# A third of the key sums moved from VectorE to accumulating DMAs of GpSimd's queue

## The chip, the cores and the metric

One core of a Trainium2 chip runs the kernel. Its engines work side by side and meet at semaphores: TensorE (PE; its weight loads are PEld), VectorE (DVE), ScalarE (ACT), GpSimd (POOL) and SyncE (SP), which here only issues DMAs. The metric is the device time of one execution in microseconds (us); smaller is better.

## The reference

Attention with a soft cap over 4 batches of 12 heads, 448 positions and 64 channels a head, and a mixer behind it. Cut to what matters:

```python
scores = scale * q @ k.T
scores = cap * tanh(scores / cap)
attn = exp(scores - max);  attn = attn / sum(attn)      # over keys
x = attn @ v                                            # heads side by side: 448 x 768
h = relu(x.T @ w_tok1) @ w_tok2;  u = x + h.T           # mixes positions
out = u + relu(u @ w_ch1) @ w_ch2                       # mixes channels
```

All is float32.

## The kernel before

Attention takes two heads (a pair `p`) at a time, with keys in the partitions. The 448 keys are cut into three full chunks of 128 (`c` = 0, 1, 2) and one of 64 (`c` = 3); the 64-key chunks of an even pair and of the odd pair after it are packed into one tile. So two pairs have seven units of work, and the 24 pairs have 84. A unit is: the score matmuls (`qk_unit`, L182 or L188), one tanh (L195) and one exponential (L200) of a 128 x 896 tile `e` on ACT, and the matmuls with v (`pv_full` L217, `pv_packed` L226).

The exponentials must also be summed over keys. `add_up` does it in two moves: DVE first adds the chunks of a pair elementwise into `acc` (128 x 2 x 448 for each of two pairs), and later `add_rows` lets PE add up the 128 partitions with a matmul by ones (L265). In `add_up`, chunk 0 + chunk 1 make `acc` (L239), chunk 2 is added in place (L245), and the packed chunk is added as two halves of 64 partitions (`add_packed`, L257). For an odd pair the packed chunk, which has been there since the even pair, is added right behind L239, before chunk 2.

The order is written out by hand. There are 42 steps with two units each. Step `t` issues the v matmuls of its own two units, then the scores, tanh and exponentials of the two units of step `t + 2`, then `add_up` for its own units, then some 1.8 us (as the program reckons) of background PE work, taken from a list: `add_rows` of two pairs, and the first half of the mixer for batches that are done (transposes L326, `tok1` L353, `tok2` L373). `at(d, f)` puts `f` off by `d` steps. Behind `add_rows` comes a chain with one step for each link: copy the sums out of PSUM (L270), gather them by DMA (L286), reciprocal (L290), store and spread them by DMA (L292, L299), and scale the pair's output (`scale_pair`, L303), which the transposes read. After attention, `while accs` makes steps without new units until the last sums are issued; then the second half of the mixer (`ch1` L552, `ch2` L569) fills the rest, with the last of the background work put between its matmuls.

Three pools of buffers tie this together. `e` has 8 buffers, so the tanh of unit `n` overwrites the tile of unit `n - 8`, and waits for all that read that tile. `acc` has 2 buffers of two pairs each. The score PSUM tile has 2 buffers. GpSimd's only steady work is a subtraction in the decoding of weights (L119), and no DMA is issued from its queue. DVE's other work in this stage is weight decoding (L99 to L116), copies out of PSUM (L270, L279) and the differences of the high and low parts (L339, L340, L362, L439).

Of the kernel before, what the change touches and what calls it, by code (L numbers as in the profile page):

```python
# [12 lines left out]
ALU = mybir.AluOpType  # L13
# [26 lines left out]
def tile_softcap_mixer(ctx, tc, qk, v, cap, w1, w2, wc1, wc2, out):  # L40
    nc = tc.nc
# [30 lines left out]
    def at(d, f, y=0):  # L72
        later.setdefault((now[0] + d, y), []).append(f)
# [80 lines left out]
    def half(i, j):  # L154
        return slice((i ^ j) * D, ((i ^ j) + 1) * D)
# [18 lines left out]
    es = {}  # L174
# [55 lines left out]
    accs = {}  # L230

    def add_up(b, p, c):
        q, i = divmod(p, 2)
        if c == 0:
            return
        if c == 1:
            if i == 0:
                accs[b, q] = pe.tile([P, 2, 2, S], F32, tag="acc", name="acc", bufs=2)
            nc.vector.tensor_tensor(accs[b, q][:, i], es.pop((b, p, 0)), es.pop((b, p, 1)), op=ALU.add)  # L239
            if i == 1:  # L240
                add_packed(b, p)
                es.pop((b, p - 1, NF))
        elif c == 2:
            t = accs[b, q][:, i]
            nc.vector.tensor_tensor(t, t, es.pop((b, p, 2)), op=ALU.add)  # L245
            if i == 1:
                left[b] += 1
                at(1, lambda: work.insert(0, (add_rows(b, q), lambda: True)))
        else:
            add_packed(b, p)  # L250

    def add_packed(b, p):
        q, i = divmod(p, 2)
        for j in range(2):
            r = half(i, j)
            t = accs[b, q][r, i, j]
            nc.vector.tensor_tensor(t, t, es[b, p - i, NF][r, i], op=ALU.add)  # L257

    def add_rows(b, q):
        ps = ps_c.tile([P, 512], F32, tag="c", name="ps_s")  # L260
        acc = accs.pop((b, q))
        for i in range(2):
            for j in range(2):
                r = (2 * i + j) * SP
                nc.tensor.matmul(ps[r:r + SP, :S], ones, acc[:, i, j], start=True, stop=True, tile_position=(0, r))  # L265
        yield 750, True

        def take():
            x = px.tile([P, S], F32, tag="xs", name="xs", bufs=1)
            nc.vector.tensor_copy(x, ps[:, :S])  # L270
            at(pace[0], lambda: gather(b, q, x))

        read_at(b, None, take)
# [8 lines left out]
    def gather(b, q, x):  # L282
        s = px.tile([P, S // SP], F32, tag="sums", name="sums", bufs=1)
        for i in range(4):
            r = slice(i * SP, (i + 1) * SP)
            nc.sync.dma_start(s[r], x[i * SP:i * SP + 1, :].rearrange("p (a c) -> p a c", a=SP))  # L286
        at(pace[0], lambda: norm(b, q, s), 1)
# [112 lines left out]
    work = []  # L400
# [3 lines left out]
    def read_at(b, f, g):  # L404
        def free():
            unread[0] -= 1
            left[b] -= 1

        if f is not None:
            at(1, f)  # L410
        at(1, g, 1)
        at(slack[0], free, 0 if slack[0] > 1 else 1)
# [80 lines left out]
    for t in range(steps_in):  # L493
# [11 lines left out]
        for b, p, c in two:  # L505
            add_up(b, p, c)
            n = pairs.index((b, p))
            if c == (2 if p % 2 else NF) and n + 3 < len(pairs):
                at(1, lambda n=n: load_v(*pairs[n + 3]))
            if b == 0 and c == 1 and tokw_steps:  # L510
                tokw_steps.pop(0)()
            if b >= 1 and p % 2 and c == 2 and w0_steps:
                w0_steps.pop(0)()
# [238 lines left out]
```

## Time and profile before

| | |
|---|---|
| Device time, 3 runs | median 607.08 us (605.6 to 607.22) |
| The profiled execution | 605.01 us, of which the span of the profile is 603.0 us |
| Granted TensorE clock | 1.00 over the whole span |
| PE, DVE, ACT, POOL busy | 592.0, 384.9, 254.5, 54.5 us |

The span runs from the first to the last instruction; 2.0 us of the profiled execution lie outside it. A "<-" behind a row's idle time names what the engine was waiting for. A busy share says how much of a stretch an engine had work in it, not whether that work was waited for.

### The profile page before, as it was taken

How to read it: one execution, taken by the hardware profiler on the slowest of the kernel's cores; microseconds unless marked ns; L12 is line 12 of the kernel's file. 1: busy time of each engine (PE TensorE's matmuls, PEld its weight loads, DVE VectorE, ACT ScalarE, POOL GpSimd, SP SyncE). 2: the span in 40 equal slices, each digit the busy share in tenths (PEclk: the TensorE clock that was granted, in tenths of full speed). 3: DMA queues.
4: the chain of work that ended last, by engine and by line, in shares of the span. 5: the costliest groups of instructions: out<-in, count | busy, mean ns of one | idle time of the engine just before them, and what ended most of it. 6: DMA issues, size and time to landing. Idle time of an engine off the chain costs nothing.

```text
span 603.0 us, 7760 instructions
## 1 busy us (share of the span) xinstructions
PE 592.0 (98%) x3012; PEld 438.2 (73%) x3012; DVE 384.9 (64%) x626; ACT 254.5 (42%) x330; POOL 54.5 (9%) x48
## 2 busy tenths in 40 slices
PE   8998999999999999999999999999999999999997
PEld 2232444444444589997999999999989999999986
DVE  2899879696996996547788386438643853333324
ACT  7998987888878733114332122012211220000000
POOL 0021000000010000002331022001200120000000
PEclk9999999999999999999999999999999999999999
DMA  6545434244442201001343121202120200000224
GB/s 202 170 127 160 148 123 152 78 158 144 135 156 81 68 31 32 0 1 36 104 124 123 34 70 59 83 0 76 66 70 1 70 1 1 1 1 0 93 100 180
DMA packets 24620, 49.12 MB, mean 81 GB/s; under 512 B 6784, under 2 KB 16512, under 8 KB 24576
## 3 DMA queue, kind: packets, MB, share of 16 engines
q1 hardware_dynamic: 24288, 48.37, 24.9%
q8 instruction: 25, 0.41, 0.3%
q14 instruction: 19, 0.16, 0.1%
q10 hardware_dynamic: 288, 0.18, 0.1%
HBM read 42.86 MB, written 5.59 MB: 80 GB/s over the span
## 4 chain that ended last, share of the span: by engine, by line
PE 89%; DVE 5%; ACT 3%; issue 1%; DMA 1%; POOL 0%; SPq 0%; DVEq 0%
PE ps_g L552 29%; PE ps_o L569 29%; PE ps_pv L217 8%; PE ps_qk L182 8%; PE ps_h L353 5%; PE ps_u L373 5%; PE ps_s L265 2%; PE ps_pv L226 2%; PE ps_qk L188 1%; PE ps_t L326 1%; ACT e L195 1%; DVE acc L257 1%; ACT e L200 1%; DVE acc L239 1%; DMA qkraw<-in_qk 1%
## 5 line engine op out<-in xcount | busy, mean ns | idle before, releaser
L569 PE MATMUL ps_o<-g,wc 128*128 128x448 f32 x864 | 182.7, 367 | 0.0
L569 PEld LDWEIGHTS ps_o<-g,wc 128*128 128x128 f32 x864 | 161.6, 188 | 15.2 <-DVE u L574 0.9
L552 PE MATMUL ps_g<-uhl,wc 128*128 128x448 f32 x648 | 138.4, 367 | 0.0
L552 PEld LDWEIGHTS ps_g<-uhl,wc 128*128 128x128 f32 x648 | 120.9, 188 | 10.3
L574 DVE TENSOR_TENSOR u<-u,ps_o 128x448 f32<-128x448 f32 (+1 forms) x145 | 86.7, 612 | 46.8 <-PE ps_o L569 46.6
L195 ACT ACTIVATE e<-ps_qk,tsc 128x896 f32<-128x896 f32 x84 | 81.1, 1022 | 27.9 <-PE ps_qk L182 25.5
L200 ACT ACTIVATE e<-e,near 128x896 f32<-128x896 f32 x84 | 83.5, 1057 | 0.0
L119 POOL TENSOR_TENSOR wc<-wz,wc 128x512 fp32r<-128x512 f32 x36 | 48.2, 1341 | 385.4 <-ACT wc L118 361.9
L557 ACT ACTIVATE g<-ps_g 128x896 fp32r<-128x896 f32 x24 | 22.0, 916 | 142.5 <-PE ps_g L552 142.5
L558 DVE SCALAR_TENSOR_TENSOR g<-ps_g,g 128x896 fp32r<-128x896 f32 x24 | 26.1, 1088 | 75.1 <-ACT g L557 75.1
L182 PE MATMUL ps_qk<-qkraw 64*128 64x448 f32 x288 | 66.1, 570 | 1.0 <-DMA qkraw<-in_qk 0.9
L217 PE MATMUL ps_pv<-e,vn 128*64 128x448 f32 x288 | 64.2, 556 | 0.5 <-ACT e L195 0.5
L182 PEld LDWEIGHTS ps_qk<-qkraw 64*128 64x128 f32 x288 | 24.0, 186 | 42.9 <-issue 12.1
L118 ACT ACTIVATE wc<-wz 128x512 fp32r<-128x512 f32 x36 | 22.7, 629 | 74.6 <-PE ps_g L552 33.9
L552 PE MATMUL ps_g<-last_u,wc 128*128 128x448 f32 x216 | 45.6, 367 | 0.4 <-PE ps_o L569 0.3
L552 PEld LDWEIGHTS ps_g<-last_u,wc 128*128 128x128 f32 x216 | 40.4, 188 | 4.7 <-issue 0.7
L104 ACT ACTIVATE wz<-wraw 128x512 f32<-128x512 f32 x36 | 24.2, 673 | 46.1 <-DMA wraw<-in_wc 27.9
L217 PEld LDWEIGHTS ps_pv<-e,vn 128*64 128x64 f32 x288 | 16.5, 135 | 33.4 <-issue 15.9
L107 DVE TENSOR_SCALAR wz<-wz 128x512 f32<-128x512 f32 (+1 forms) x40 | 17.4, 435 | 34.8 <-ACT wz L104 34.7
L353 PEld LDWEIGHTS ps_h<-wc,last_u 128*128 128x128 f32 x176 | 30.4, 188 | 8.0 <-issue 6.0
L353 PE MATMUL ps_h<-wc,last_u 128*128 128x384 f32 x176 | 36.0, 343 | 0.0
L373 PE MATMUL ps_u<-last_u,wc 128*128 128x448 f32 x144 | 34.1, 375 | 1.5 <-DVE wc L362 0.8
(50 smaller groups left out, 414.3 us busy)
## 6 DMA issues: line engine op xcount, KB each, us to landing
wraw<-in_wc SPq DMA_DIRECT2D x36, 512.0 KB, 3.6
qkraw<-in_qk SPq DMA_DIRECT2D x23, 448.0 KB, 3.3
vn<-in_v SPq DMA_DIRECT2D x24, 224.0 KB, 3.4
rb<-rs SPq DMA_DIRECT2D x48, 112.0 KB, 2.8
out_t<-u SPq DMA_DIRECT2D x23, 224.0 KB, 1.9
wraw<-in_w SPq DMA_DIRECT2D x2, 512.0 KB, 4.7
wraw<-in_w SPq DMA_DIRECT2D x2, 448.0 KB, 3.7
sums<-xs SPq DMA_DIRECT2D x48, 1.8 KB, 2.3
```

What stands on the lines that cost most here:

```text
L104: nc.scalar.activation(zf, bits(r[:, :, 1]), AF.Abs, scale=2.0 ** -16)
L119: nc.gpsimd.tensor_tensor(lo, zf, hi, op=ALU.subtract)
L182: nc.tensor.matmul(ps[:, j, :S], raw[r, 1, c * P:(c + 1) * P], raw[r, 0], start=True, stop=True)
L195: nc.scalar.activation(e, scores.pop((b, p, c))[:, :, :S], AF.Tanh, scale=tsc)
L200: nc.scalar.activation(e, e, AF.Exp, scale=near)
L217: nc.tensor.matmul(ps[j * D:(j + 1) * D, :S], vn[p % 3][:, j * NF + c], es[b, p, c][:, j], start=first, stop=last)
L353: nc.tensor.matmul(ps[:, :HALF], w, x, start=(n == 0), stop=(n == len(mm) - 1))
L373: nc.tensor.matmul(ps[:, :S], h1[:, hi, t, cs], w2s[:, wi, t, :], start=(n == 0), stop=(n == 3 * NT - 1))
L552: nc.tensor.matmul(ps[:, i, :S], w[:, wi, cc, fs], uhl[b][:, ui, cc, :], start=(n == 0), stop=(n == 3 * NC - 1))
L558: nc.vector.scalar_tensor_tensor(g[:, 1], ps[:, :, :S], 0.0, g[:, 0], op0=ALU.max, op1=ALU.subtract)
L569: nc.tensor.matmul(ps[:, :S], w[:, wi, i, cs], g[:, gi, i, :], start=(n == 0), stop=(n == 3 * GF - 1))
L574: nc.vector.tensor_tensor(u[b][:, cc, r], u[b][:, cc, r], ps[:, r], op=ALU.add)
```

## The change

The third key chunk of each pair is no longer added by DVE (L245). A DMA issued from GpSimd's queue reads the 128 x 896 tile `e`, adds it to `acc` and writes `acc` (`accum_op=ALU.add`). For an odd pair it is issued where L245 stood; for an even pair it is issued one unit later, behind the packed chunk's two additions. `add_rows` is put into the list two steps after the odd pair's third chunk, where it was one step.

```diff
         elif c == 2:
-            t = accs[b, q][:, i]
-            nc.vector.tensor_tensor(t, t, es.pop((b, p, 2)), op=ALU.add)
             if i == 1:
+                add_third(b, p)
                 left[b] += 1
-                at(1, lambda: work.insert(0, (add_rows(b, q), lambda: True)))
+                at(2, lambda: work.insert(0, (add_rows(b, q), lambda: True)))
         else:
             add_packed(b, p)
+            add_third(b, p)
+
+    def add_third(b, p):
+        q, i = divmod(p, 2)
+        nc.gpsimd.dma_start(accs[b, q][:, i], es.pop((b, p, 2)), accum_op=ALU.add)
```

## Rows read from the trace of the kernel before

**Rows 1.** Busy time, share of the span and instructions of each engine.

```profile
PE 592.0 (98%) x3012; PEld 438.2 (73%) x3012; DVE 384.9 (64%) x626; ACT 254.5 (42%) x330; POOL 54.5 (9%) x48
```

**Rows 2.** Stretch, its length, busy us of PE, PEld, DVE, ACT, POOL; clock, DMA share.

```profile
8.83:49.72 40.89, 40.44 (x218) 11.66 (x216) 34.84 (x53) 40.89 (x46) 3.19 (x3) 1.00 0.47 152
49.72:208.43 158.71, 154.97 (x848) 70.11 (x847) 131.67 (x216) 131.77 (x162) 10.32 (x8) 1.00 0.41 129
208.43:283.56 75.13, 74.12 (x390) 65.50 (x389) 49.95 (x91) 25.24 (x47) 4.06 (x3) 1.00 0.07 20
```

**Rows 3.** Instructions that touch `acc`: count, ns min/median/max, first and last start.

```profile
L257 DVE TENSOR_TENSOR acc<-acc,e x48: 606/622/1355, 13.7 to 211.9; 64x448 f32<-64x448 f32 x48
...
L245 DVE TENSOR_TENSOR acc<-acc,e x24: 1020/1091/1120, 12.5 to 212.6; 128x896 f32<-128x896 f32 x24
```

**Rows 4.** Groups of instructions by line: count, busy us, mean ns, idle before them.

```profile
L195 ACT ACTIVATE e<-ps_qk,tsc 128x896 f32<-128x896 f32 x84 | 81.1, 1022 | 27.9 <-PE ps_qk L182 25.5 <-PE ps_qk L188 2.3
...
L119 POOL TENSOR_TENSOR wc<-wz,wc 128x512 fp32r<-128x512 f32 x36 | 48.2, 1341 | 385.4 <-ACT wc L118 361.9 <-issue 17.9 <-PE ps_o L569 5.6
```

**Rows 5.** Waits of PE between 46 and 215 us: total, times, longest.

```profile
PE ps_t L326 <- DVE u L303: 1.9, 1, 1.9
PE ps_t L326 <- DVE wc L340: 0.9, 2, 0.7
...
PE ps_s L265 <- DVE wc L340: 0.4, 1, 0.4
```

**Rows 6.** Timeline from 49 us, the first transposes: start, length, engine, line.

```profile
49.72 2.00 ACT L195 ACTIVATE e<-ps_qk,tsc 128x896 f32<-128x896 f32 x2
...
51.57 1.15 DVE L303 TENSOR_TENSOR u<-xr,rb 128x448 f32<-128x448 f32 x2
...
52.33 1.10 PE L326 MATMUL ps_t<-ident,u 128*128 128x128 f32 x8 [1.87 <-DVE u L303]
...
56.08 1.91 ACT L195 ACTIVATE e<-ps_qk,tsc 128x896 f32<-128x896 f32 x2 [1.54 <-PE ps_qk L182]
```

**Rows 7.** Timeline from 28 to 46 us, ahead of those transposes.

```profile
28.16 0.62 DVE L270 COPY xs<-ps_s 128x448 f32<-128x448 f32 x1 [1.11 <-PE ps_s L265]
...
30.48 1.39 POOL L119 TENSOR_TENSOR last_u<-wz,last_u 128x512 fp32r<-128x512 f32 x1 [29.10 <-DVE last_u L116]
...
30.77 1.39 DVE L108 TENSOR_SCALAR wz<-wz 128x512 int32<-128x512 int32 x1
...
35.82 1.09 DVE L245 TENSOR_TENSOR acc<-acc,e 128x896 f32<-128x896 f32 x1
...
38.43 0.96 PE L265 MATMUL ps_s<-acc,ones 128*32 128x448 f32 x8
...
43.25 1.08 DVE L245 TENSOR_TENSOR acc<-acc,e 128x896 f32<-128x896 f32 x1
```

**Rows 8.** Timeline, release and reuse of two of the third-chunk buffers.

```profile
25.98 2.01 ACT L200 ACTIVATE e<-e,near 128x896 f32<-128x896 f32 x2
...
35.13 1.96 ACT L195 ACTIVATE e<-ps_qk,tsc 128x896 f32<-128x896 f32 x2
...
44.44 1.25 DVE L257 TENSOR_TENSOR acc<-acc,e 64x448 f32<-64x448 f32 x2
```

**Rows 9.** Timeline, the last two pairs' sums.

```profile
211.26 1.26 DVE L257 TENSOR_TENSOR acc<-acc,e 64x448 f32<-64x448 f32 x2
...
216.75 0.96 PE L265 MATMUL ps_s<-acc,ones 128*32 128x448 f32 x8
```

**Rows 10.** DMA issues: count, KB each, median us from issue to landing.

```profile
qkraw<-in_qk SPq DMA_DIRECT2D x23, 448.0 KB, 3.3
...
out_t<-u SPq DMA_DIRECT2D x23, 224.0 KB, 1.9
...
sums<-xs SPq DMA_DIRECT2D x48, 1.8 KB, 2.3
...
out_t<-u SPq DMA_DIRECT2D x1, 112.0 KB, 1.7
```

## The prediction

> **What bounds the kernel now.** I read the busy times first: PE has work in 592.0 of 603.0 us [rows 1], so no more than 11 us of PE's idle time can be had anywhere. Whether the attention stage has any of it, and who causes it, is told by the stretches [rows 2]. From 8.8 to 49.7 us ACT is busy in all of its 40.89 us: the tanh and exponential of two units, four instructions like the L195 of 1.02 us [rows 4], make a step: the tanh of four steps apart start at 35.13 and 49.72 us [rows 6, 8], 3.65 us for each step. DVE, with 34.8 us, is second there. From 49.7 to 208.4 us the background work has begun: 31 steps take 158.7 us, 5.1 us each, PE is busy in 155.0 and idle in 3.7, and ACT and DVE have some 27 us to spare. So the stage is first ACT's and then PE's. DVE matters only where its queue has fallen behind. The waits of PE [rows 5] show what that costs: 1.9 us once, where the first transposes wait for `scale_pair`, and 1.3 us in three places where a PSUM bank is waited for that DVE's L340 had still to read. Together 3.2 of the 3.7 us.
>
> **What it removes.** 24 L245 of 1.09 us [rows 3] are 26.2 us of DVE, in a stage where DVE is not the bound. It is worth only what DVE's lateness costs PE. The first transposes run at 52.33 us after a wait of 1.87 us for L303, which started at 51.57 [rows 6]. DVE last stood idle at 28.16 us; between there and L303 it does two L245, at 35.82 and 43.25 us [rows 7]. Without them L303 comes 2.2 us earlier and the wait is gone. But step 10, which takes 56.08 - 49.72 = 6.36 us from tanh to tanh [rows 6], can't become shorter than ACT's 3.65, and since the sums come a step later the first transposes (1.10 us) move to step 11, where PE has to do them after all. 6.36 - 3.65 - 1.10 = 1.6 us are left. Of the 1.3 us of bank waits I take half, 0.7: L340 stands behind ACT's L333 as well as in DVE's queue. An earlier evacuation copy, too, is hidden by ACT before 49.7 us and by the list of background work after it. Gain: 2.3 us; the bounds are 0 (other waits end at the same time) and all of the 3.7 us.
>
> **What it adds.** 24 DMAs of 448 KB, each with a latency that I call L, from the moment when DVE and ACT have finished its operands to its landing. The trace has no accumulating DMA and none from GpSimd. Its nearest rows [rows 10]: 448 KB from HBM land in 3.3 us, 224 KB out of SBUF in 1.9 and 112 KB in 1.7, 1.8 KB from SBUF to SBUF in 2.3. So a pass over 448 KB is some 0.8 us by the stores (0.2 us for each 112 KB) and the fixed part is 1.5 to 2.3 us. An accumulation must read two operands and write one. For the issue by GpSimd I take one of its instructions over all partitions, 1.34 us [rows 4]. Lower bound: L is 3.3 us, a plain load. Upper bound: three whole loads one after the other and the issue, 3 x 3.3 + 1.3 = 11.2. I take the fixed part, three passes and the issue: 2.1 + 3 x 0.8 + 1.3 = 5.8 us, nearer to the lower end since the passes can run on 16 engines at once, whose busy share is 0.47 and 0.41 here [rows 2]. The 24 issues cost GpSimd some 32 us; its subtractions L119 fill only 13.5 of the 200 us [rows 2], and an L119 queued behind a waiting DMA is late by at most that wait, with a step or more until its reader.
>
> **Who waits for L.** Three kinds of reader. *The tanh that takes the buffer of the third chunk, eight units on.* The DMA of an even pair waits for the packed additions. For pair 2 the packed tile's exponential is the first of the two that start at 25.98, so it ends at 27.0; DVE adds it in 1.25 us, to 28.3 us once L270 and its wait are no longer ahead; the tanh that reuses the buffer is the second of those at 35.13, at 36.1 [rows 8]. Cover: 7.8 us. For pair 4 the additions end at 45.69 [rows 8], less 2.2 us for the two L245 and 1.0 us for the moved L270 and its wait [rows 7]; the tanh starts at 49.72 [rows 6]. Cover: 7.2 us. The odd pairs' DMAs wait for nothing that comes later and have more. Here ACT has no slack, so each us over the cover is a us lost; from 49.7 us on, ACT runs ahead of PE by most of a step. *L265*, which is now a step later, 3.65 us and afterwards 5.1. For pairs 2 and 3 it starts at 38.43, 1.5 us behind the L245 that started at 35.82 [rows 7]; the DMA can start where that did, so the cover is 1.09 + 1.5 + 3.65 = 6.2 us. *The last L265*: the last packed additions end at 212.5 and L265 runs at 216.75 [rows 9], 4.2 us, and one more turn of `while accs` with up to 1 us of background work makes 5.2. With L = 5.8 PE waits 0.6 us there. At the end nothing else is later: the loop takes one turn more, and the chain behind the sums is counted in steps after it.
>
> **The sum.** The profiled execution is 605.01 us, 603.0 of span and 2.0 around it: 603.0 - 1.6 - 0.7 + 0.6 = 601.3 of span, 603.3 with the rest. The median of the runs is 607.08, 2.07 above that execution, so I forecast 607.08 - 1.7 = 605.4 us. With all of the 3.7 us gained and nothing lost at the end it is 603.4.
>
> **GpSimd and DVE share something.** DVE's L108 took 1.39 us from 30.77 us; GpSimd's L119 ran until 31.87, and L108 ended 0.3 us behind it [rows 7]. So it lay 1.1 us beside an instruction that held it up. The longest L257 took 1.36 us where the median is 0.62 [rows 3]. The Trainium skill ("SBUF — State Buffer", Who interferes with whom) says that VectorE's two-port operations and GpSimd's descriptor writing lock each other out for whole instructions, while a two-input add does not stop descriptor writing. L108's row agrees with the lock; no run here shows the descriptors.
>
> **The rivals.**
> (A) *The gain is hidden anyway.* ACT sets the first 50 us and PE the rest, and the 1.9 us wait is taken over by the next latest thing, ACT's exponentials or the DMA that brings `rb`. For it: ACT has no idle time before 49.7 us [rows 2]. Against: PE waits for DVE by name [rows 5]. With no gain and 0.6 us at the last sums: 607.1 to 607.7 us.
> (B) *The accumulation is slow, and ACT waits for the buffer.* It decides from the L at which the three covers' excess equals the gain: (L - 5.2) + (L - 7.2) + (L - 7.8) = 2.3, L = 7.5 us. At L = 8.5 it is 5.3 us lost and 2.3 gained, 610.1 us; at 10, 9.8 lost, 614.6 us. For it: two streams read and one written through engines that the loads keep busy to 0.47 in the very stretch with the small covers [rows 2]. Against: the rows of SBUF transfers give 5.8.
> (C) *GpSimd's issues hold DVE up.* If each of the 24 issues blocks a DVE instruction as L119 did L108, 24 x 1.1 us = 26 us come back, all that was saved, DVE stays as late as it is, and the issues that wait in turn for a run of DVE instructions of 1 to 2 us make L 7 to 8 us. No gain, 1.8 to 2.8 us at the last sums and up to 1.0 at the two buffers: 608.9 to 610.9 us, and 607.5 where the locks are short. The Trainium skill ("SBUF — State Buffer", A bandwidth-pool intuition that's wrong) gives an example in which a transfer starved of descriptors takes 3.1 in place of 0.62 us; by it an estimate of L is 5.8 + 2.5 = 8.3 us, 4.7 us lost, and the time 609.5 us with the gain and 611.8 without.
>
> **How the numbers follow.** A measurement here tells from no change what is over 0.3%, 1.8 us: faster is below 605.26, slower above 608.90. The forecast (chance 0.45) lies just at that bound, 603.4 to 606; its bigger part, 0.32, I put on the faster side, since covers on the last sums may be larger than I counted, and 0.13 on the same. (A) 0.21: same 0.18, faster 0.03. (B) 0.19: slower 0.17, same 0.02. (C) 0.15: slower 0.09, same 0.04, faster 0.02. Faster 0.37, same 0.37, slower 0.26. The likeliest time is 605.4, the sum above. The range starts 0.9 us under the 603.4 of the full gain, since the runs shown lie 1.6 us apart, and ends at 610.5, between (B) at L = 8.5 and the upper end of (C): 602.5 to 610.5 leaves out the greater half of (B), about 0.12, and 0.05 below.
>
> **What the profile would show.** Right: L245 gone and DVE's busy time down by 26 us; step cadence 3.65 us up to 53.4 and no wait of L326 for L303; 24 issues from GpSimd's queue that land in 5 to 7 us; no wait of L195 on a DMA. (A) shows the waits of PE renamed, not gone. (B) shows "ACT e L195 <- DMA acc" near 36 and 50 us, and L265 waiting for a DMA. (C) shows DVE's instructions stretched beside GpSimd's. What would make it wrong above all is L: the trace before has no row for it.

## The result, and the profile after

The changed kernel takes 612.7 us (median of 4 runs, 611.86 to 613.24), the one before 607.15: a ratio of 1.0099 [1.0079, 1.0120], some 6 us slower (5.5 by the medians), where 605.4 was forecast and 610.5 was the end of the range. The profiled execution is 613.13 us with a span of 611.4. Lines move by 4: L257 is now L261, L265 is L269, L303 is L307, L326 is L330, L340 is L344; the accumulating DMA is L254. (In the experiments lines move by other amounts.)

The busy times of the page, which answer to [rows 1], show that the planned exchange took place. DVE lost 24 instructions and 24.3 us. POOL gained 24 and 20.5 us. PE, with the same 3012 instructions, is busy for 4.4 us longer; it isn't given more work, it is slower or stuck in some of it.

```profile
PE 596.4 (98%) x3012; PEld 439.4 (72%) x3012; DVE 360.6 (59%) x602; ACT 255.3 (42%) x330; POOL 75.0 (12%) x72
```

PE's waits between 5 and 220 us (from 46 to 215 in [rows 5]): the 1.9 us for L303 that the prediction wanted to remove are gone. Two others stand in their place, both in the sums over keys.

```profile
PE ps_s L269 <- ACT wc L337: 3.5, 3, 1.4
PE ps_s L269 <- DMA acc<-e: 2.3, 1, 2.3
PE ps_t L330 <- DVE wc L344: 1.1, 2, 1.0
```

DVE waited for no DMA in this stage before. Now it does, for 21.8 us in all; its waits over the same stretch:

```profile
DVE sums L294 <- DMA sums<-xs: 12.8, 5, 5.6
...
DVE wz L99 <- DMA wraw<-in_w: 6.4, 2, 3.5
DVE u L307 <- DMA rb<-rs: 2.6, 1, 2.6
```

The DMA issues of the page, to be read beside [rows 10]: the accumulations land 5.1 us after their issue in the median, and the 448 KB loads in 3.9 where they took 3.3.

```profile
acc<-e POOLq DMA_DIRECT2D x24, 448.0 KB, 5.1
qkraw<-in_qk SPq DMA_DIRECT2D x23, 448.0 KB, 3.9
```

By source line the landings spread from 4.2 to 9.6 us, and an issue costs GpSimd 0.86 us:

```profile
L254 POOL DMA_DIRECT2D acc<-e x24: 862/864/1125, 15.5 to 218.3; - x24
...
DMA to landing us min/median/max: 4.2/5.1/9.6
```

The 9.6 us is one transfer, the eighth, of batch 1's second pair. The timeline of the changed kernel from 64 us tells its story. SP issues two loads of 448 and 512 KB at 64.58 and 65.90; GpSimd issues the accumulation at 66.29, right behind them. The matmuls of L269 begin with the half that is there, and the other four stand until 75.95. The PV group behind them (L217, eight matmuls) takes 3.23 us, where the same group took 1.72 at 64.49.

```profile
64.49 1.72 PE L217 MATMUL ps_pv<-e,vn 128*64 128x448 f32 x8
64.58 1.27 SPq L167 DMA_DIRECT2D qkraw<-in_qk  x1
...
65.90 1.06 SPq L91 DMA_DIRECT2D wraw<-in_wc  x1
...
66.29 0.86 POOL L254 DMA_DIRECT2D acc<-e  x1 [2.64 <-DVE u L307]
...
68.89 0.63 DVE L307 TENSOR_TENSOR u<-xr,rb 128x448 f32<-128x448 f32 x1 [2.62 <-DMA rb<-rs]
...
69.33 1.74 PE L226 MATMUL ps_pv<-e,vn 64*64 64x448 f32 x8
...
70.11 0.20 PEld L226 LDWEIGHTS ps_pv<-e,vn 64*64 64x64 f32 x4 [0.58 <-DVE xr L283]
...
72.71 0.95 PE L269 MATMUL ps_s<-acc,ones 128*32 128x448 f32 x4
73.12 0.67 ACT L104 ACTIVATE wz<-wraw 128x512 f32<-128x512 f32 x1 [1.60 <-DMA wraw<-in_wc]
...
75.95 1.08 PE L269 MATMUL ps_s<-acc,ones 128*32 128x448 f32 x4 [2.30 <-DMA acc<-e]
76.67 0.24 DVE L294 RECIPROCAL sums<-sums 128x14 f32<-128x14 f32 x1 [5.62 <-DMA sums<-xs]
...
76.96 3.23 PE L217 MATMUL ps_pv<-e,vn 128*64 128x448 f32 x8
```

A second wait lies ahead of it, inside a row: the eight matmuls of L226 take 1.74 us, since the second four stand for a PSUM bank that DVE frees late (L283), behind L307 and its wait of 2.62 us for a small DMA.

By stretches (columns as in [rows 2]) the 16 DMA engines are at 0.99 of their time while the transfer is under way, PE is busy in 2.70 of 5.00 us, and in the 5 us after the wait the granted clock is 0.69: partly the 1.2 GHz level in place of 2.4. (The share goes by the packets' times and can come out over 1, as it does further down.)

```profile
64.00:72.00 8.00, 8.00 (x46) 2.81 (x40) 4.38 (x7) 7.28 (x8) 0.86 (x1) 1.00 0.99 252
72.00:77.00 5.00, 2.70 (x16) 0.38 (x12) 0.33 (x2) 3.88 (x6) 0.00 (x0) 0.96 0.79 218
77.00:82.00 5.00, 5.00 (x19) 1.58 (x18) 4.83 (x9) 1.73 (x3) 0.86 (x1) 0.69 0.31 66
```

### The profile page after: what moved, and what is told of

It is laid out like the page before. It is cut to its first block, busy times and chain, and to the rows that moved or that the text cites. A ratio compares the mean times of both kernels' runs of the same rounds, so it can differ in the third digit from the quotient of the medians.

```text
span 611.4 us, 7815 instructions
## 1 busy us (share of the span) xinstructions
PE 596.4 (98%) x3012; PEld 439.4 (72%) x3012; DVE 360.6 (59%) x602; ACT 255.3 (42%) x330; POOL 75.0 (12%) x72
## 4 chain that ended last, share of the span: by engine, by line
PE 73%; DVE 8%; DMA 7%; ACT 6%; issue 3%; SPq 1%; POOL 1%; DVEq 0%; ACTq 0%; POOLq 0%
PE ps_o L573 24%; PE ps_g L556 24%; PE ps_pv L217 6%; PE ps_h L357 5%; PE ps_qk L182 5%; PE ps_u L377 5%; DMA wraw<-in_wc 3%; DMA acc<-e 2%; ACT e L195 2%; ACT e L200 2%; PE ps_s L269 1%; DVE wz L111 1%; DVE wz L112 1%; DMA wraw<-in_w 1%; PE ps_qk L188 1%
## 5 line engine op out<-in xcount | busy, mean ns | idle before, releaser
L195 ACT ACTIVATE e<-ps_qk,tsc 128x896 f32<-128x896 f32 x84 | 80.9, 1012 | 31.3 <-PE ps_qk L182 23.3
L217 PE MATMUL ps_pv<-e,vn 128*64 128x448 f32 x288 | 65.5, 567 | 0.8 <-ACT e L200 0.8
L217 PEld LDWEIGHTS ps_pv<-e,vn 128*64 128x64 f32 x288 | 16.8, 138 | 34.7 <-issue 17.4
L107 DVE TENSOR_SCALAR wz<-wz 128x512 f32<-128x512 f32 (+1 forms) x40 | 18.8, 471 | 33.1 <-ACT wz L104 32.9
L254 POOL DMA_DIRECT2D acc<-e x24 | 21.3, 888 | 126.9 <-ACT e L195 27.9
```

The costliest lines, as they stand in the source:

```text
L195: nc.scalar.activation(e, scores.pop((b, p, c))[:, :, :S], AF.Tanh, scale=tsc)
L217: nc.tensor.matmul(ps[j * D:(j + 1) * D, :S], vn[p % 3][:, j * NF + c], es[b, p, c][:, j], start=first, stop=last)
```

## The experiments

Sixteen kernels were run. The ratio is to the kernel before, run beside it on the same chip; the number of runs stands behind the median. What is called tanh below is L195, and a step's tanh the first of its two.

```
kernel                                              us          ratio [95%]
e1_step       before, sums two steps behind         607.10 (10) 1.0005 [0.9993, 1.0018]
e6_none_one   before, no third chunk                605.52 (8)  0.9965 [0.9950, 0.9981]
e2_none_step  after, no third chunk                 606.72 (10) 1.0001 [0.9986, 1.0016]
e3_copy       after, copies, not accumulations      607.59 (10) 1.0016 [1.0002, 1.0030]
e5_one        after, sums one step behind           624.33 (4)  1.0291 [1.0266, 1.0316]
e4_three      after, sums three steps behind        610.05 (7)  1.0067 [1.0046, 1.0088]
e8_odd        after, odd pairs alone by DMA         610.34 (4)  1.0062 [1.0039, 1.0085]
e9_traffic    before, 18 transfers nobody needs     608.31 (10) 1.0021 [1.0006, 1.0035]
e10_pace      after, reciprocal a step later        616.70 (4)  1.0151 [1.0132, 1.0170]
e11_scale     before, scale_pair first in its step  611.55 (6)  1.0058 [1.0036, 1.0080]
e12_defer     after, one sum a step later           611.96 (4)  1.0093 [1.0061, 1.0124]
e13_one_dve   after, one addition back on DVE       608.47 (10) 1.0025 [1.0012, 1.0039]
e14_even      before, even pairs by DMA             607.26 (10) 0.9999 [0.9987, 1.0012]
e15_single    before, one addition by DMA           605.75 (12) 0.9985 [0.9971, 0.9998]
e16_pool_one  before, one addition by GpSimd        607.74 (12) 1.0015 [1.0000, 1.0030]
e17_pool_even before, even pairs by GpSimd          612.17 (6)  1.0089 [1.0070, 1.0109]
```

### Is the gain there, and what does the later step cost?

e1_step: the step alone.

```
-                at(1, lambda: work.insert(0, (add_rows(b, q), lambda: True)))
+                at(2, lambda: work.insert(0, (add_rows(b, q), lambda: True)))
```

> The kernel before with the sums over keys two steps behind and all additions still on VectorE. Theory 1 (the later place of the sums costs: the matmuls by ones now follow the transposes and wait for a PSUM bank that ScalarE and VectorE have still to read): the three waits of 1.1 to 1.5 us ahead of the matmuls by ones at 58, 97 and 135 us are here too, nothing is saved on VectorE, and the time is 2 to 4 us over the kernel before (609 to 611). Theory 2 (the accumulating transfers alone cost): no such waits of over 0.5 us, time within 1 us of the kernel before (606 to 608).

e6_none_one: the kernel before without the additions of the third chunk.

```
-            t = accs[b, q][:, i]
-            nc.vector.tensor_tensor(t, t, es.pop((b, p, 2)), op=ALU.add)
+            es.pop((b, p, 2))
```

> The kernel before with its 24 additions of the third chunk left out (that chunk is missing in the sums) and everything else in its old place, the sums one step behind. It prices the gain by itself. The prediction's sum: the wait of 1.9 us of the first transposes for VectorE is gone and some of the bank waits, 2 to 3 us less than the kernel before (0.995 to 0.997). Rival: VectorE's time is worth nothing, whatever the step, since ScalarE's instruction between the transposes and VectorE ends last: 0.999 to 1.001.

e2_none_step: the changed kernel without the transfers.

```
-        nc.gpsimd.dma_start(accs[b, q][:, i], es.pop((b, p, 2)), accum_op=ALU.add)
+        es.pop((b, p, 2))
```

> The changed kernel without its accumulating transfers; the third chunk is left out of the sums. It has the changed kernel's order and its saved VectorE time, and no transfers. Theory 1: still 609 to 611, since the waits ahead of the matmuls by ones stay. Theory 2: 603.5 to 605.5, the gain that was forecast, and the whole difference to the changed kernel (612.7) is the transfers'. In both, the gaps of 0.17 us inside the matmuls by ones are gone if they come from a second wait on a transfer.

The step alone costs nothing (+0.05%), as theory 2 wanted, though two of theory 1's three bank waits are there (2.6 us in all). Without the additions and with the old step the kernel gains 0.35%, 2.1 us [1.2, 3.0]: the gain of 2.3 was there. With both, nothing is left (+0.01%), a time between the ranges of the two theories. PE's waits of the kernel without additions at the old step, and then at the new one, say why:

```profile
PE ps_s L264 <- DVE wc L339: 1.0, 2, 0.6
PE ps_t L325 <- DVE wc L339: 0.9, 2, 0.7
```

```profile
PE ps_s L269 <- DVE wc L344: 3.0, 3, 1.5
PE ps_t L330 <- DVE wc L344: 1.1, 2, 1.0
```

A step later the sums come behind the transposes and want a PSUM bank of the same pool, which is only free when DVE has evacuated the transposes: 1.0 us of bank waits become 3.0. So 2 us are lost before a single byte is transferred. The twelve groups of L269 take 0.96 us each here, as those of L265 did before. In the changed kernel three of them take longer, at 43.06 (1.05), 72.71 (4.32 with its wait) and 222.01 us (1.50): these gaps go with the transfers.

### What do the transfers cost?

e3_copy moves the same bytes without adding.

```
-        nc.gpsimd.dma_start(accs[b, q][:, i], es.pop((b, p, 2)), accum_op=ALU.add)
+        nc.gpsimd.dma_start(accs[b, q][:, i], es.pop((b, p, 2)))
```

> The changed kernel with the 24 transfers as plain copies over the sums, in the same places with the same waits; what chunks 0, 1 and 3 had summed up is overwritten. If it is the accumulation (a second operand read) that makes the transfers slow, their median from issue to landing falls from 5.1 us to under 4 and the longest from 9.6 to under 7, and the time falls by 2 us or more to 609 to 611. If it is the crowd of loads on the same engines and the issue by GpSimd, the landing stays at 4.5 to 5.1 us, the longest over 8, and the time stays within 1.5 us of 612.7.

607.59 us, 0.9 above the kernel without transfers and under both ranges; the accumulation costs 5.1 us more. The copies land in 2.7 to 6.7 us, median 3.8, and an issue takes GpSimd 0.56 us. The longest is again the eighth, and it holds the same matmuls: the group takes 2.07 us in place of 0.96, and the 1.1 us more cover all that this kernel loses.

```profile
70.56 0.95 PE L269 MATMUL ps_s<-acc,ones 128*32 128x448 f32 x4
...
71.68 0.95 PE L269 MATMUL ps_s<-acc,ones 128*32 128x448 f32 x4 [0.18 <-DMA acc<-e]
```

The rows of GpSimd's queue (packets, MB, share of 16 engines), of the copies and then of the changed kernel: 4.7% of 605.0 us is 1.18 us of all engines for each transfer, 9.9% of 611.4 is 2.52.

```profile
q0 software_dynamic: 1920, 11.01, 4.7%
```

```profile
q0 software_dynamic: 3456, 11.01, 9.9%
```

e5_one and e4_three move the sums back to one step and on to three.

```
-                at(2, ...)
+                at(1, ...)     # e5_one; at(3, ...) in e4_three
```

> The changed kernel with the sums one step behind, where they stood before. Covers of the matmuls by ones are a step shorter, 1.5 to 3 us. If landings that outlast the cover are the cost, several of the twelve matmuls by ones wait for a transfer, 1 to 4 us each, and the time is 618 to 630. If the transfers cost mostly by traffic and by ScalarE's buffers, it is 612 to 615.

> The changed kernel with the sums over keys three steps behind. If late landings make the matmuls by ones wait, the wait of 2.6 us near 73 us and the lower clock behind it are gone, 3 to 4 us less than the changed kernel (609 to 610). If the place among the transposes decides, the waits move to other places and the time is 611 to 614, with the wait for the PSUM bank still named.

At one step PE waits for the transfers for 9.4 us, three times, at a mean clock of 0.989:

```profile
PE ps_s L269 <- DMA acc<-e: 9.4, 3, 3.7
```

At three steps there is no such wait, though the eighth transfer lands after 9.8 us there too. By the medians 2.65 us come back (1.9 by the ratios, whose intervals overlap); 3.3 over the kernel without transfers stay. Two things share these, and the run doesn't divide them: ACT's tanh now waits 5.7 us for transfers that hold its buffer, 3.4 in the changed kernel, and everything behind the sums is a step later at the end of the stage.

e8_odd sends half of the transfers.

```
         elif c == 2:
-            if i == 1:
+            if i == 0:
+                t = accs[b, q][:, i]
+                nc.vector.tensor_tensor(t, t, es.pop((b, p, 2)), op=ALU.add)
+            else:
                 add_third(b, p)
...
             add_packed(b, p)
-            add_third(b, p)
```

> The changed kernel with the third chunk of even pairs added by VectorE where it stood before and only the odd pairs' twelve by accumulating transfers. The odd pairs' buffers and sums have the larger covers. If the cost comes from landings that outlast the cover, most of it is gone: no wait of ScalarE's tanh for a transfer, and 606.5 to 608.5. If each transfer costs its share by its traffic, half of the cost stays: 609 to 610.5.

610.34 us. No tanh and no matmul waits for an accumulation by name (ACT's L444 does once, 2.4 us at 218.76), and still 3.6 us are lost over the kernel without transfers, 2 of them in one bank wait at 61.74 us: DVE had stood 2.06 us for the small DMA of the sums, and its evacuation came late. That spoke for a cost that grows with the number of transfers; e14_even, below, speaks against it.

```profile
58.13 0.24 DVE L296 RECIPROCAL sums<-sums 128x14 f32<-128x14 f32 x1 [2.06 <-DMA sums<-xs]
...
61.74 0.58 PE L271 MATMUL ps_s<-acc,ones 128*32 128x448 f32 x4 [1.97 <-DVE wc L346]
```

### Traffic alone, and DVE's waits alone

e9_traffic adds to the kernel before (cut to the two instructions):

```
...
+        nc.gpsimd.tensor_copy(mark, accs[b, p // 2][:, i, 0, :1])
+        nc.gpsimd.dma_start(u[B - 1][:, 2 * i:2 * i + 2], u[B - 1][:, 4:6], accum_op=ALU.add)
```

> The kernel before, unchanged in what it computes, with 18 accumulating transfers of 448 KB of zeros within a buffer that nobody needs yet (batches 0 to 2), issued from GpSimd at the changed kernel's moments behind a one-column GpSimd copy that reads the accumulator. Nobody waits for their data. Theory 1 (the transfers cost by the share of the DMA engines that they take from the loads and from the small DMAs of the sums): 2 to 4 us slower, 609 to 611, and DVE's waits for sums, rb and wraw, none before, come to 8 us and more. Rival (they cost only where somebody waits for their landing): within 0.15% of before, 606.2 to 608.

+0.21%, some 1.3 us: less than theory 1 wanted, more than the rival; DVE's waits for DMAs come to 4.5 us, where theory 1 wanted 8. Its profile shows one event in the whole stage. A weight load lands late, DVE stands for it, its copy L289 that frees a PV bank is late, and PE waits 3.16 us:

```profile
44.43 0.39 DVE L100 TENSOR_SCALAR wz<-wraw 128x448 int32<-128x448 int32 x1 [2.06 <-DMA wraw<-in_w]
...
49.38 0.62 DVE L289 COPY xr<-ps_pv 128x448 f32<-128x448 f32 x1
...
50.09 1.76 PE L218 MATMUL ps_pv<-e,vn 128*64 128x448 f32 x4 [3.16 <-ACT e L201]
```

(The profile names ACT, whose exponentials ended at 49.68; the copy's end, 50.00, fits the start better.) From the next step to the stage's end its tanh instructions stay 3.3 to 3.6 us (4.7 in one step) behind those of the kernel before, whose profiled execution lies 2 us under its median: the transfers of the next 150 us cost nothing that lasts.

e10_pace takes DVE off its waits for the sums.

```
-        at(pace[0], lambda: norm(b, q, s), 1)
+        at(2, lambda: norm(b, q, s), 1)
```

> The changed kernel, with the reciprocal of the sums two steps behind the DMAs that spread them and not one, so that DVE doesn't stand behind a late small DMA. Theory 1a (the delayed small DMAs cost through DVE, which waits for them in order and so is late for its evacuation copies): DVE's waits for sums fall from 12.8 us to under 4 and the time falls by 1.5 to 3 us, to 610 or 611. Rival (DVE's waits are slack; the waits for the landings themselves and PE's bank waits set the time): 612 to 613.5, as the changed kernel.

The waits for the sums fall from 12.8 to 3.0 us as meant, and the kernel takes 4 us more, over both ranges. PE's wait for the accumulation near 73 us is there as before, 3.3 us, and PE's waits for banks did not fall with DVE's. So theory 1a's gain did not come. The run doesn't price DVE's waits by themselves: it makes the chain behind the sums a step longer, so that twelve fewer matmuls have run by the last tanh (1029 against 1041) and are left for the time behind it.

### One landing

Set beside the kernel without transfers, the tanh of equal steps show where the time goes (starts in us, from the traces; these four have the same order of matmuls):

```
step            8      10      14      15      16      17    last
e2_none_step  42.23   49.80   66.08   70.75   74.40   79.89  200.98
e3_copy       42.20   49.78   66.03   71.46   75.28   80.93  201.96
after         42.76   51.17   67.42   74.17   81.20   86.85  207.92
e13_one_dve   42.30   50.47   66.71   72.01   75.66   81.11  202.16
```

The changed kernel is 1.3 us late at step 14, 7.0 at step 17, and 6.9 at the end. So 5.6 us arise between 66 and 87 us, around the transfer that took 9.6. The same matmuls of the kernel without transfers, set beside the timeline above, divide them:

```profile
68.00 0.98 PE L226 MATMUL ps_pv<-e,vn 64*64 64x448 f32 x8
...
70.61 0.96 PE L269 MATMUL ps_s<-acc,ones 128*32 128x448 f32 x8
...
71.50 1.72 PE L217 MATMUL ps_pv<-e,vn 128*64 128x448 f32 x8
```

L226 takes 0.8 us more in the changed kernel. From the start of L269 to that of L217 it is 4.25 us in place of 0.89, which is 3.4 more: the wait of 2.3, and two half groups, one behind the other. L217 takes 1.5 more. That makes 5.6. Two kernels test whether the one landing is the cause.

e12_defer keeps the transfer and lets one sum come later; e13_one_dve takes the one transfer away.

```
-                at(2, ...)
+                at(3 if (b, q) == (1, 0) else 2, ...)          # e12_defer
```

```
-                add_third(b, p)
+                if (b, p) == (1, 1):                            # e13_one_dve
+                    t = accs[b, q][:, i]
+                    nc.vector.tensor_tensor(t, t, es.pop((b, p, 2)), op=ALU.add)
+                else:
+                    add_third(b, p)
```

> The changed kernel with all its 24 transfers, only the sums over keys of batch 1's first two pairs three steps behind, not two: those whose matmul waited 2.3 us for a transfer that landed 9.6 us after its issue. Theory 1 (nearly all of the loss is that one landing: the wait, the low clock that follows it and the loads that were late with it): 4 us and more come back, 607.3 to 609 us. Rival (24 transfers each cost a little, through the loads and through DVE's waits): the one wait's 2.3 us at most come back, and the rest stays, 610.5 to 612.

> The changed kernel with one of the 24 additions back on DVE, that of batch 1's second pair, whose transfer landed 9.6 us after its issue; the other 23 go by DMA. Theory 1 (that one landing is nearly all of the loss): 607.3 to 609 us. Rival (24 transfers each cost a little): 1/24 of the loss of 6 us comes back, 612.2 to 612.7.

With 23 transfers in place of 24 the kernel takes 608.47 us: 4.2 of the 6.0 us come back for one addition. In the table its offset grows by 0.6 us at that place and no longer by 5.6 (the late bank of L226 is still there, at 1.59 us), and in the same stretches PE is busy throughout at a clock of 1.00:

```profile
72.00:77.00 5.00, 5.00 (x29) 2.08 (x23) 4.50 (x9) 5.00 (x7) 0.86 (x1) 1.00 0.44 114
77.00:82.00 5.00, 5.00 (x30) 2.23 (x28) 4.07 (x8) 3.69 (x5) 0.86 (x1) 1.00 1.08 248
```

e12_defer, which takes away the wait and leaves the transfer, came out at 611.96, with runs from 610.63 to 615.16: by its number the rival's. PE's wait for the transfer is gone there, though it lands after 9.3 us, behind the same loads. But the background work falls in another order, and another landing holds a tanh instead, with a wait of PE of 2.2 us behind it:

```profile
101.18 1.01 ACT L195 ACTIVATE e<-ps_qk,tsc 128x896 f32<-128x896 f32 x1 [2.86 <-DMA acc<-e]
```

That wait of PE is about what its profiled execution, the fastest of the four, has over e13_one_dve's (2.0 us); what the slower three lost has no trace. So a reader moved out of one landing's way can meet the next.

### Can the gain be had?

e11_scale moves DVE's `scale_pair` ahead of the additions.

```
-        at(pace[0], lambda: scale_pair(b, p, rb), 2)
+        at(pace[0], lambda: scale_pair(b, p, rb), 1)
```

> The kernel before, with the additions on DVE and only scale_pair's place in its step changed: ahead of the step's additions, not behind them. If the 1.9 us that the first transposes wait for scale_pair were a matter of DVE's order alone, the wait falls to under 0.5 us and the time by 1 to 2 us, to 605 to 606. If ACT sets that step anyway, or scale_pair then makes an evacuation late, no change within 0.1%: 606.5 to 607.7.

Slower by 0.58%, which neither case wanted: DVE now waits for `rb` there, six times, 7.5 us in all, where it waited for no DMA, and PE still waits 2.1 us for it.

e14_even and e15_single start from the kernel before, at one step; e15_single has `(b, p) == (0, 4)` for `i == 0`.

```
+            if not (i == 0):
                 t = accs[b, q][:, i]
                 nc.vector.tensor_tensor(t, t, es.pop((b, p, 2)), op=ALU.add)
...
             add_packed(b, p)
+            if i == 0:
+                nc.gpsimd.dma_start(accs[b, q][:, i], es.pop((b, p, 2)), accum_op=ALU.add)
```

> The kernel before, with its sums over keys one step behind, where only the twelve even pairs' third chunks are added by accumulating transfers, which have a whole pair's steps to land before the sums read them; the odd pairs' stay on DVE. Theory 1 (a transfer costs only where its landing, or a load that it makes late, holds an engine up in order): half of DVE's relief is worth about 1 us, less up to 0.6 for late loads: 606 to 607 us, and no matmul waits for a transfer. Rival (transfers cost by their number): as the kernel with the odd pairs' twelve, 609 to 610.5 us.

> The kernel before with one of its 24 additions, that of batch 0's fifth pair at 43.25 us, done by an accumulating transfer; everything else as before. Of the 1.9 us for which the first transposes waited for DVE, 1.1 go with that addition: 605.7 to 606.5 us if DVE's lateness there was the cause and nothing takes its place; 606.9 to 607.5 if the wait is only renamed or the loads beside the transfer are late.

Twelve transfers whose sums are far cost nothing that shows (0.9999): PE waits for none of them, so it isn't their number. They bring nothing either, since the tanh at 51.75 waits 1.95 us for a buffer that a transfer still reads, and the transposes wait 1.87 us for DVE as before. The single transfer is the best of all that add the third chunk, 605.75 us, ratio 0.9985 [0.9971, 0.9998]; that is half of what a measurement of this kernel tells from no change. Its time lies in the first range, but its trace shows only half of the reason: the wait for DVE falls by 0.5 us, not 1.1, and a wait of 1.0 for a bank appears.

e16_pool_one and e17_pool_even do the same additions by GpSimd, without transfers.

```
-                nc.gpsimd.dma_start(accs[b, q][:, i], es.pop((b, p, 2)), accum_op=ALU.add)
+                t = accs[b, q][:, i]
+                nc.gpsimd.tensor_tensor(t, t, es.pop((b, p, 2)), op=ALU.add)
```

> The kernel before with one addition, that of batch 0's fifth pair, done by a GpSimd instruction behind the packed additions, without any transfer. If the loads beside the transfer took away what the one transfer gave, this gives more than that one: 605 to 606 us, with the first transposes waiting 0.8 us or less. If the wait is renamed whatever carries the addition: 606.3 to 607.5.

> The kernel before with the twelve even pairs' third chunks added by GpSimd instructions behind the packed additions; no transfers. If DVE's relief pays wherever no transfer crowds the loads: 605 to 606.3 us. If GpSimd's two-operand additions hold DVE's instructions up, or are so slow that the tanh waits for the buffer: 607 us and more, with DVE's instructions stretched beside them.

The second is slower by 0.89%; the first's 0.15% [1.0000, 1.0030] is hardly told from no change. In the first, GpSimd's addition takes 2.43 us, and DVE's L112, which starts beside it, 2.40 us where the same shape otherwise takes 0.62. The 1.08 us taken off DVE cost it 1.78.

```profile
44.34 2.43 POOL L254 TENSOR_TENSOR acc<-acc,e 128x896 f32<-128x896 f32 x1 [2.55 <-DVE acc L261]
...
44.85 2.40 DVE L112 SCALAR_TENSOR_TENSOR wz<-wraw,wz 128x448 int32<-128x448 int32 x1
```

In the second, twelve additions take GpSimd 27.4 us, and the mean of `scale_pair` on DVE (L307) is 1095 ns where it was 665 with the one, as in the kernel before.

## Why the prediction was wrong

Two steps failed: the gain of 2.3 us that the moved sums were to leave standing, of which nothing was left, and the one value of L, 5.8 us, held against the cover of L265 in the loop, where one landing of 9.6 us went through. What the trace before had no row for was L, and the prediction had named that as its weakest term.

**What bounds the kernel.** Right in the main: PE, with some 2 us to be had from DVE's lateness (2.1 measured without the additions). But the reading of the first stretch names DVE as second behind ACT, and the same row has PE busy in 40.44 of its 40.89 us.

**What it removes.** The 2.3 us were there with the sums one step behind, and the change moves them. The prediction priced the moved step at 1.1 us of transposes and counted half of the bank waits as gain. In fact add_rows came behind the transposes and waited for the bank that they held, 3.0 us in place of 1.0. This term failed by the whole gain. It failed as a combination, since the step alone was free (607.10 us). There the wait for L303 fell from 1.9 to 1.0 us while the bank waits of the sums rose from 0.4 to 2.6; these rows don't balance, and why that step is free stays open.

**What it adds.** L was 5.8 us, and the median landing is 5.1 from the issue. What failed is that one value stood for 24 transfers. They land in 4.2 to 9.6 us. The longest was issued 0.4 and 1.7 us behind two big loads, and the same transfer landed late in four kernels: after 9.6 us here, 9.3 in e12_defer, 9.8 in e4_three and 9.4 in e10_pace. The Trainium skill ("DMA: Bandwidth & Descriptors", Issuing engines are not separate DMA queues) states that transfers run on the same 16 engines and interleave, whichever engine issued them. The trace agrees that they share: those two loads landed after 6.6 and 7.1 us, where the medians of their kind are 3.9 and 3.6. Two loads ahead and a full share are not enough for a late landing, though. The transfer at 106.22 has as much ahead of it, 2.1 and 1.7 us before, and the engines' share is 1.04 until it lands, 4.74 us after its issue.

```profile
104.09 0.33 SPq L167 DMA_DIRECT2D qkraw<-in_qk  x1
104.51 0.40 SPq L91 DMA_DIRECT2D wraw<-in_wc  x1
...
106.22 0.86 POOL L254 DMA_DIRECT2D acc<-e  x1 [3.75 <-DVE acc L261]
```

What goes with late landings is loads issued at nearly the same moment. The ten traces with accumulating transfers have 186 of them. The 145 that have no load of 448 or 512 KB issued within 1 us before or behind land after 4.9 us in the median (4.2 to 7.6), the 21 with one after 6.0 (5.2 to 9.6), the 20 with two after 7.9 (6.4 to 9.8). That is a count over traces as they are; no run moved the loads.

**Who waits for L.** This is the step that decided. The cover of L265 in the loop was set at 6.2 us and counted as safe against 5.8; the one landing of 9.6 went through it. By its own rows that cover was 7.4 us from the issue (PE stood from 73.65), so 2.3 us were left to wait. The rows account for the 5.6 us that arise there: 3.4 from the split sums with that wait in them, 1.5 of slow matmuls behind it, and 0.8 in front, where a small DMA landed late, DVE's copy was late behind it and PE wanted the bank. The landing itself thus stands for 4.9; of the 0.8, 0.6 stay in e13_one_dve. The tanh that reuses the buffer waited where the prediction feared it, at 51.17, but for 0.65 us. Three others wait for transfers too, the longest 1.93 us at 106.13; the right outcome was to show none. In e13_one_dve such a wait, 2.00 us at 100.46, leaves no mark on the later steps.

**At the end nothing else is later.** The 0.6 us at the last L265 came, inside a row: the last group of L269 takes 1.50 us where it took 0.96 [rows 9], because its second four stand for the last transfer.

```profile
222.01 1.50 PE L269 MATMUL ps_s<-acc,ones 128*32 128x448 f32 x8
...
222.56 0.14 PEld L269 LDWEIGHTS ps_s<-acc,ones 128*32 128x32 f32 x4 [0.41 <-DMA acc<-e]
222.63 1.04 ACT L442 ACTIVATE uhl<-u 128x448 fp32r<-128x448 f32 x2 [2.26 <-DMA acc<-e]
```

That the size fits is partly luck. The last additions end at 217.76 and the transfer lands at 222.5, so L was 4.8 us and not 5.8, and the cover was as much shorter. The sentence itself is not right: with the sums a step later, ten fewer matmuls have run by the last tanh (1041 against 1051) and are left for the time behind it. No cost of that shows in e1_step.

**The rivals.** (B) was nearest in time, 610.1 at L = 8.5, but not as written: its median never came near the 7.5 us from which it was to decide, and the last sums and the small covers paid little. (A) held for what it says of the gain, with another heir than the ones it named: a PSUM bank. (C) is refuted at its price of 26 us: DVE's additions L261 take 617 ns in the mean (645 before), L108 grew from 522 to 604 ns over ten, and DVE in all lost 24.3 of the 26.2 us. The estimate of 8.3 us for a transfer starved by DVE is not what the median shows.

**Still open.** The cost of 24 transfers without that landing is 1.8 us (608.47 against 606.72). By the table 0.6 of it arise before step 10 and 0.6 between steps 14 and 15, where L226 waits for its bank; the rest lies behind the last tanh, where the last sums wait. Late small DMAs and loads that hold DVE in order are shown in one place each, by e13_one_dve and e9_traffic; how far they make the rest isn't. That the loads issued beside it made that one transfer late is only counted, above, and was not tested by moving them.

## What to carry to other kernels

For transfers that share the engines with big loads, don't hold a median against the cover: hold the longest landing against the reader that is nearest, and look first at transfers with big loads issued within 1 us of them. One of 24 made 4.2 of 6 us here, one with as much issued a little earlier landed in half the time, and twelve whose sums were far cost nothing that shows. Look for waits inside the rows, too: a group that takes longer than its like hides one (1.50 us for 0.96, 1.74 for 0.98). Where a change both relieves an engine and moves a step, price the two together, since the moved step's new neighbours (here a shared PSUM pool) can take the whole relief.

## What the hardware showed that was not expected

- Adding in the DMA costs about twice the engines' time of copying: 2.52 against 1.18 us of all 16 engines for 448 KB, 144 against 80 packets for each, 0.86 against 0.56 us of GpSimd for the issue, and a median landing of 5.1 against 3.8 us.
- Behind a wait of 2.3 us the next eight matmuls of PE took 1.5 us more than their like, while the granted clock was 0.69 from 77 to 82 us; from 64 to 72 us it was 1.00. In e10_pace, behind the wait of 3.3 us at the same place, it was 0.66 over the same stretch.
- A two-operand addition of 128x896 floats takes GpSimd 2.28 us in the mean (DVE 1.09), and DVE's L112 beside it took 2.40 us in place of 0.62. The Trainium skill ("SBUF — State Buffer", Who interferes with whom) states that a VectorE instruction with two SBUF inputs contends with a GpSimd instruction that reads SBUF; L112 reads `wraw` and `wz`, and the trace agrees.
